# FFN work per iteration derived from TensorE's attention steps, in a top-k attention kernel with a SwiGLU block behind it

## The chip, the cores and the metric

The kernel runs on one core of a Trainium2 chip. Times are device microseconds of one execution. Before the change the median of three runs is 1890.77 us (1890.12 to 1893.95). The profile is of one execution of 1892.5 us.

## The reference

Eight batches with eight heads each attend over 576 positions of 64 numbers. Of each row of scores only the 32 largest count. The result, laid out as 4608 tokens of 512 numbers, goes through a gated FFN.

```python
def _attn_ref(q, k, v):                      # q, k, v: (8, 8, 576, 64)
    scores = scale * np.matmul(q, k.transpose(0, 1, 3, 2))
    kth = np.partition(scores, -top_k, axis=-1)[..., -top_k:-top_k + 1]
    mask = scores >= kth                     # top_k = 32
    scores = np.where(mask, scores, -1000000000.0)
    scores = scores - np.max(scores, axis=-1, keepdims=True)
    attn = np.exp(scores)
    attn = attn / (np.sum(attn, axis=-1, keepdims=True) + 1e-09)
    return np.matmul(attn, v).astype(np.float32)

def _moe_ref(x, w_gate, w_val, w_out):       # x: (4608, 512), d_ff 1536
    g = x @ w_gate
    silu = g * (1.0 / (1.0 + np.exp(-g)))
    val = x @ w_val
    return (silu * val @ w_out).astype(np.float32)
```

## The kernel before

The program is one long sequence. It is cut into 160 units: batch, query tile, pair of heads. Tiles 0 to 3 hold 128 queries, and such a unit has two rows of scores per partition, one for each head. Tile 4 (`qt == J`) holds the last 64 queries; the two heads share the partitions, and there is one row.

```python
units = [(b, qt, hp) for b in range(B) for qt in range(J + 1) for hp in range(NHP)]   # J = 4, NHP = 4

def n_heads(qt):
    return 1 if qt == J else 2
```

The main loop is a software pipeline over the units. In iteration n VectorE selects the 32 largest of unit n, while TensorE transposes the weights of unit n - 3 (`turn`), multiplies those of unit n - 4 with v (`values`), and makes the scores of unit n + 1 (`scores`). Before a new batch it also transposes keys and queries (`fetch`, for unit n + 2 with `qt == 0`). All engines take their instructions in the order in which the loop writes them down.

```python
TURN, VALUES = 3, 4
for n in range(NU + VALUES):                 # NU = 160
    nh = n_heads(units[n][1]) if n < NU else 1
    ...
    if n >= NU - NHP:
        credit[0] = 8.0
    else:
        credit[0] = min(credit[0] + (4.45 if nh == 2 else 2.25), 8.0)
    flush(on_act)
    if 0 <= n - 1 < NU:
        penalize(n - 1)                      # GpSimd
    flush(on_pool)
    if 0 <= n - TURN < NU:
        run(turn(n - TURN))                  # TensorE transposes, ScalarE copies
    if n >= VALUES:
        finish_unit(n - VALUES)              # TensorE: weights times v
    next(nxt, None)                          # TensorE: scores of n + 1
    if 0 <= n - 1 < NU:
        weigh(n - 1)                         # ScalarE: exp
    run(nxt)                                 # ScalarE: copies of the scores
    dve(2, beside=False)                     # VectorE: steps of select(n)
    ...
    pieces(2)
    ...
    dve(1)
    dve(1)
    next(norm, None)                         # VectorE: 1 / sum of unit n - 2
    run(norm)                                # ScalarE: weights of unit n - 2, scaled
    next(ahead, None)                        # TensorE: keys and queries of a new batch
    pieces(1)
    next(ahead, None)
    dve(1)
    pieces(1)
    dve(2)
    run(topk)
    pieces(6)
while piece():
    pass
```

Beside attention, TensorE works through the FFN in pieces. A piece of the gate or value product is four matmuls and costs 1 credit; a piece of the output product, which is done in seven quarter products, is three matmuls and costs 0.75. A block of 256 tokens has 24 pieces of the first kind and 14 of the second (block 0: 12 pieces of the plain output product, at 1 each). A block can begin only when all its tokens have their attention. Where no block is ready, `piece()` returns 0 and the credit is kept, up to 8.

```python
def pieces(n):
    for _ in range(n):
        if credit[0] >= 1:
            credit[0] -= piece()

def piece():
    ...
    while True:
        if not current:
            if not todo or done.get(todo[0], 0) < NHP * BLK:   # BLK = 256
                return 0
            ...
            current.append(feed(todo.pop(0)))
        cost = next(current[0], 0)
        ...
        return cost
```

The instructions that the profile names by line: 297 and 283 are the matmuls of scores of a full and a half unit, 302 and 288 the ScalarE copies of these scores out of PSUM; 318 is VectorE's maximum of eight, the first of which in a unit reads the scores (`m<-sc`), and 322 its replacement of what was found; 340 is GpSimd's adding of the penalty; 349 exp and 364 the scaling of the weights, both on ScalarE; 376 the transposes of weights; 396 and 405 weights times v; 459 the gate and value products; 545 the quarter products of the output.

Of the kernel before, what the change touches and what calls it, by code (L numbers as in the profile page):

```python
# [27 lines left out]
def kernel(  # L28
# [40 lines left out]
    J = S // P  # L69
# [64 lines left out]
    def weights():  # L134
# [11 lines left out]
        for n in range(len(pieces) + lags[0]):  # L146
            for lag in lags:
                if 0 <= n - lag < len(pieces):
                    next(pieces[n - lag], None)
            ready[0] = max(n - lags[0] + 1, 0)  # L150
            yield
# [38 lines left out]
    def rounding(n):  # L190
        for _ in range(n):
            next(weight, None)
# [9 lines left out]
    def load(i):  # L202
        b, hp = pairs[i]
        h = slice(2 * hp, 2 * hp + 2)
        kq = ld.tile([P, 2, J, 2, D], FP32, tag="kq", name="kq_in")
        kq_last = ld.tile([P, 2, D], FP32, tag="kql", name="kq_last")
        for n, src in ((0, k), (1, q)):
            queue = nc.scalar if n == 1 and i == 0 else nc.sync
            for hh in range(2):
                queue.dma_start(  # L210
                    kq[:, n, :, hh, :],
                    src[b, 2 * hp + hh, 0:JP].rearrange("(p j) d -> p j d", j=J),
                )
            queue.dma_start(
                kq_last[n * R : (n + 1) * R], src[b, h, JP:S].rearrange("h p d -> p h d")
            )
        raw[i] = (kq, kq_last)
# [42 lines left out]
    units = [(b, qt, hp) for b in range(B) for qt in range(J + 1) for hp in range(NHP)]  # L260
    state = {}

    def n_heads(qt):

        return 1 if qt == J else 2

    def scores(n):
        b, qt, hp = units[n]
        slab = preps[b * NHP + hp]
        sc = work.tile([P, 2 * S], FP32, tag="sc", name="sc", bufs=2)  # L270
        halves = [slice(0, D), slice(D, P)]
        half = S // 2

        def bank():
            return ps_t.tile([P, 512], FP32, tag="t", name="s")


        if qt == J:
            banks = [bank() for _ in range(2)]
            for i, ps in enumerate(banks):  # L280
                for d in halves:
                    k0 = R + i * half
                    nc.tensor.matmul(  # L283
                        ps[d, 0:half], slab[d, S + R : S + 2 * R], slab[d, k0 : k0 + half]
                    )
            yield
            for i, ps in enumerate(banks):
                nc.scalar.copy(sc[:, i * half : (i + 1) * half], ps[:, 0:half])  # L288
        else:
            q0 = S + 2 * R + qt * P  # L290
            banks = []
            for i in range(2):
                for hh, d in enumerate(halves):
                    ps = bank()
                    banks.append((i + 2 * hh, ps))
                    k0 = (1 - hh) * R + i * half
                    nc.tensor.matmul(  # L297
                        ps[:, 0:half], slab[d, q0 : q0 + P], slab[d, k0 : k0 + half]
                    )
            yield  # L300
            for i, ps in banks:
                nc.scalar.copy(sc[:, i * half : (i + 1) * half], ps[:, 0:half])  # L302
        state[n] = dict(sc=sc)

    def select(n):

        nh = n_heads(units[n][1])
        sc = state[n]["sc"]
        m = small.tile([P, 2, TOP_K], FP32, tag="m", name="m", bufs=2)
        heads = [slice(t * S, (t + 1) * S) for t in range(nh)]  # L310
        rest = work.tile([P, 2 * S], FP32, tag="rest", name="rest", bufs=1)
        e = work.tile([P, 2 * S], FP32, tag="e", name="e", bufs=4)
        state[n] |= dict(m=m, e=e, heads=heads)
        cur = sc
        rounds = TOP_K // 8
        for r in range(rounds):
            for t, hs in enumerate(heads):
                nc.vector.max(m[:, t, 8 * r : 8 * r + 8], cur[:, hs])  # L318
                yield
            if r < rounds - 1:  # L320
                for t, hs in enumerate(heads):
                    nc.vector.match_replace(  # L322
                        rest[:, hs], m[:, t, 8 * r : 8 * r + 8], cur[:, hs], LOWEST
                    )
                    yield
                cur = rest
        for t, hs in enumerate(heads):
            nc.vector.tensor_scalar(  # L328
                e[:, hs], sc[:, hs], m[:, t, TOP_K - 1 : TOP_K], FAR, ALU.is_lt, ALU.mult
            )  # L330

    def penalize(n):

        st = state[n]
        sc, m, e, heads = st.pop("sc"), st.pop("m"), st["e"], st["heads"]
        nh = len(heads)
        bias = small.tile([P, 2], FP32, tag="bias", name="bias")
        nc.gpsimd.tensor_scalar_mul(bias[:, 0:nh], m[:, 0:nh, 0], -scale)
        every = slice(0, nh * S)
        nc.gpsimd.tensor_tensor(e[:, every], e[:, every], sc[:, every], ALU.add)  # L340
        st["bias"] = bias
# [15 lines left out]
    def normalize(n):  # L357
        st = state[n]
        tot, e, heads = st.pop("tot"), st["e"], st.pop("heads")
        nh = len(heads)  # L360
        nc.vector.reciprocal(tot[:, 0:nh], tot[:, 0:nh])  # L361
        yield
        for t, hs in enumerate(heads):
            nc.scalar.mul(e[:, hs], e[:, hs], tot[:, t : t + 1])  # L364
# [76 lines left out]
    def flush(queue):  # L441
        while queue:
            queue.pop(0)()
# [182 lines left out]
    NU = len(units)  # L626
# [3 lines left out]
    def piece():  # L630

        if len(on_act) > 1:
            flush(on_act)
        if len(on_pool) > 1:
# [3 lines that stand above are left out]
                if not todo or done.get(todo[0], 0) < NHP * BLK:  # L638
# [5 lines that stand above are left out]
            if cost == 0:  # L644
                current.pop()
                continue
            return cost

    def fetch(n):

        b, qt, hp = units[n]
        i = b * NHP + hp
        if qt == 0:
            yield from prep(i)
        if qt == J and i + NHP < len(pairs):
            load(i + NHP)

    def pieces(n):
        for _ in range(n):
            if credit[0] >= 1:  # L660
                credit[0] -= piece()

    def run(steps):
        for _ in steps:
            pass

    def finish_unit(n):
        values(n)
        b, qt, hp = units[n]
        if qt == J and b + 1 < B:  # L670
            load_v((b + 1) * NHP + hp)
# [7 lines left out]
    credit = [0.0]  # L679
    no = iter(())  # L680
    over = {}
    TURN, VALUES = 3, 4
    due = [0.0]
    for n in range(NU + VALUES):
        nh = n_heads(units[n][1]) if n < NU else 1
        topk = select(n) if n < NU else no
        over[n - 1] = normalize(n - 1) if 0 <= n - 1 < NU else no
        nxt = scores(n + 1) if n + 1 < NU else no
        ahead = fetch(n + 2) if n + 2 < NU else no
        norm = over.pop(n - 2, no)  # L690

        def dve(k, beside=True):

            for _ in range(k * nh):
                next(topk, None)
                due[0] += 5 / 11 if beside else 0
                if due[0] >= 1:
                    due[0] -= 1
                    rounding(1)

        if n >= NU - NHP:
            credit[0] = 8.0
        else:
            credit[0] = min(credit[0] + (4.45 if nh == 2 else 2.25), 8.0)
        flush(on_act)
        if 0 <= n - 1 < NU:
            penalize(n - 1)
        flush(on_pool)
        if 0 <= n - TURN < NU:
            run(turn(n - TURN))  # L710
        if n >= VALUES:
            finish_unit(n - VALUES)
        next(nxt, None)
        if 0 <= n - 1 < NU:
            weigh(n - 1)
        run(nxt)

        dve(2, beside=False)
        if 2 <= n + 2 < NHP:
            load(n + 2)  # L720
        if n < NHP:
            load_v(n)
# [5 lines that stand above are left out]
        next(norm, None)  # L728
        run(norm)
# [8 lines that stand above are left out]
# [50 lines left out]
```

## Time and profile before

| | before |
|---|---|
| median of 3 runs | 1890.77 us |
| span of the profiled execution | 1892.5 us |
| granted TensorE clock, mean | 0.955 |
| MAX8 over scores or rest (line 318) | 1152 instructions, 615.2 + 205.4 us |
| gate and value matmuls (line 459) | 3456 records, 404.8 + 397.9 us |
| output product's quarters (line 545) | 1428 records |

In the page's first part each engine has its busy time, its share of the span and its count of instructions: PE is TensorE's matmuls, PEld its weight loads, DVE VectorE, ACT ScalarE, POOL GpSimd. In the second part each digit is the busy share of one fortieth of the span in tenths, and PEclk is the clock that TensorE was granted. A line of the list of waits reads: the engine and line that waited, the engine and line that ended the wait, microseconds in all, how often, the longest. A line of the timeline gives the start and length of a run of like instructions, and in brackets the idle time before it and what ended it.

### The profile page before, as it was taken

How to read it: one execution, taken by the hardware profiler on the slowest of the kernel's cores; microseconds unless marked ns; L12 is line 12 of the kernel's file. 1: busy time of each engine (PE TensorE's matmuls, PEld its weight loads, DVE VectorE, ACT ScalarE, POOL GpSimd, SP SyncE). 2: the span in 40 equal slices, each digit the busy share in tenths (PEclk: the TensorE clock that was granted, in tenths of full speed). 3: DMA queues.
4: the chain of work that ended last, by engine and by line, in shares of the span. 5: the costliest groups of instructions: out<-in, count | busy, mean ns of one | idle time of the engine just before them, and what ended most of it. 6: DMA issues, size and time to landing. Idle time of an engine off the chain costs nothing.

```text
span 1892.5 us, 30875 instructions
## 1 busy us (share of the span) xinstructions
PE 1723.2 (91%) x10756; PEld 1419.1 (75%) x10756; DVE 1632.0 (86%) x3477; ACT 1212.3 (64%) x3015; POOL 1023.2 (54%) x1007
## 2 busy tenths in 40 slices
PE   3446789989999999899899999999999999899998
PEld 2335658868888878787788888878888878787877
DVE  7998789999999989997899989999899989999300
ACT  5656666667666666675667666766676767666531
POOL 4555656636455546555364655554646554546534
PEclk7668899989999999899999999999999999999989
DMA  7222212000300012000210003000210001000000
GB/s 186 84 84 78 67 27 69 1 12 2 78 12 12 1 28 64 12 1 13 52 38 1 12 3 82 7 12 1 53 38 12 1 14 46 18 1 12 1 12 12
DMA packets 111260, 59.67 MB, mean 32 GB/s; under 512 B 89088, under 2 KB 97280, under 8 KB 111104
## 3 DMA queue, kind: packets, MB, share of 16 engines
q1 hardware_dynamic: 109904, 57.41, 11.6%
q8 instruction: 85, 1.39, 0.3%
q14 instruction: 71, 0.58, 0.1%
q10 hardware_dynamic: 1200, 0.30, 0.1%
HBM read 48.23 MB, written 9.44 MB: 30 GB/s over the span
## 4 chain that ended last, share of the span: by engine, by line
PE 79%; ACT 7%; POOL 7%; DVE 4%; issue 2%; DMA 0%; SPq 0%; POOLq 0%; ACTq 0%
PE f L459 38%; PE av L405 8%; PE x_ps L545 8%; PE etps L376 8%; PE s L297 6%; PE y_ps L545 5%; POOL e L340 3%; ACT e L349 2%; PE s L283 2%; ACT sc L302 2%; PE av L396 1%; DVE m L318 1%; DVE rest L322 1%; PE kqps L252 1%; PE o_ps L505 1%
## 5 line engine op out<-in xcount | busy, mean ns | idle before, releaser
L318 DVE MAX8 m<-rest 128x8 f32<-128x576 f32 x864 | 615.2, 747 | 2.2
L322 DVE MATCH_REPLACE8 rest<-m,rest 128x576 f32<-128x576 f32 x576 | 423.9, 742 | 0.0
L340 POOL TENSOR_TENSOR e<-e,sc 128x1152 f32<-128x1152 f32 (+1 forms) x160 | 382.7, 2392 | 59.4 <-DVE e L328 59.0
L459 PE MATMUL f<-xT,wg 128*128 128x256 f32 x1728 | 404.8, 385 | 0.0
L459 PE MATMUL f<-xT,wv 128*128 128x256 f32 x1728 | 397.9, 381 | 0.0
L459 PEld LDWEIGHTS f<-xT,wg 128*128 128x128 f32 x1728 | 324.4, 191 | 66.7 <-issue 23.7
L459 PEld LDWEIGHTS f<-xT,wv 128*128 128x128 f32 x1728 | 324.3, 190 | 55.6 <-issue 13.5
L487 POOL TENSOR_TENSOR h<-h,half_g 128x512 f32<-128x512 f32 x108 | 138.0, 1278 | 385.9 <-ACT h L486 377.4
L318 DVE MAX8 m<-sc 128x8 f32<-128x576 f32 x288 | 205.4, 749 | 127.1 <-ACT sc L288 70.9
L376 PE MATMUL etps<-ident,e 128*128 128x128 f32 (+1 forms) x1312 | 191.0, 291 | 132.2 <-POOL size L116 48.1
L349 ACT ACTIVATE e<-e,bias 128x576 f32<-128x576 f32 x288 | 222.0, 776 | 114.6 <-POOL e L340 114.6
L376 PEld LDWEIGHTS etps<-ident,e 128*128 128x128 f32 (+1 forms) x1312 | 161.9, 150 | 163.9 <-POOL size L116 51.3
L377 ACT COPY et<-etps 128x512 f32<-128x512 f32 (+1 forms) x448 | 185.0, 483 | 126.5 <-PE etps L376 124.9
L492 POOL TENSOR_TENSOR h<-h,val 128x512 f32<-128x512 f32 x108 | 140.0, 1296 | 160.8 <-ACT val L491 160.8
L364 ACT ACTIVATE e<-e,tot 128x576 f32<-128x576 f32 x288 | 211.5, 787 | 5.3 <-DVE tot L361 5.1
L322 DVE MATCH_REPLACE8 rest<-m,sc 128x576 f32<-128x576 f32 x288 | 211.8, 741 | 0.0
L297 PE MATMUL s<-kqT 64*128 64x288 f32 x1024 | 175.5, 451 | 9.1 <-ACT kqT L257 5.8
L328 DVE TENSOR_SCALAR e<-sc,m 128x576 f32<-128x576 f32 x288 | 173.4, 639 | 3.4
L405 PE MATMUL av<-et,v 128*64 128x128 f32 (+1 forms) x2560 | 176.3, 284 | 0.0
L302 ACT COPY sc<-s 128x288 f32<-128x288 f32 x512 | 163.9, 402 | 3.3 <-PE s L297 3.3
L484 ACT ACTIVATE h<-f 128x512 f32<-128x512 f32 x108 | 65.2, 603 | 149.8 <-PE f L459 149.8
L405 PEld LDWEIGHTS av<-et,v 128*64 128x64 f32 x2560 | 139.2, 147 | 23.4 <-issue 7.9
(71 smaller groups left out, 2042.6 us busy)
## 6 DMA issues: line engine op xcount, KB each, us to landing
kq_in<-in_k_dram SPq DMA_DIRECT2D x64, 128.0 KB, 2.8
v<-in_v_dram SPq DMA_DIRECT2D x32, 256.0 KB, 3.0
kq_in<-in_q_dram SPq DMA_DIRECT2D x62, 128.0 KB, 2.9
w<-in_moe_w_gate_dram SPq DMA_DIRECT2D x24, 256.0 KB, 2.7
w<-in_moe_w_val_dram SPq DMA_DIRECT2D x24, 256.0 KB, 2.7
w<-in_moe_w_out_dram SPq DMA_DIRECT2D x24, 256.0 KB, 2.6
out_dram<-o SPq DMA_DIRECT2D x40, 128.0 KB, 2.4
out_dram<-o SPq DMA_DIRECT2D x16, 256.0 KB, 2.4
```

Of the source, the lines that this page charges most:

```text
L297: nc.tensor.matmul(ps[:, 0:half], slab[d, q0 : q0 + P], slab[d, k0 : k0 + half])
L302: nc.scalar.copy(sc[:, i * half : (i + 1) * half], ps[:, 0:half])
L318: nc.vector.max(m[:, t, 8 * r : 8 * r + 8], cur[:, hs])
L322: nc.vector.match_replace(rest[:, hs], m[:, t, 8 * r : 8 * r + 8], cur[:, hs], LOWEST)
L340: nc.gpsimd.tensor_tensor(e[:, every], e[:, every], sc[:, every], ALU.add)
L349: nc.scalar.activation(e[:, hs], e[:, hs], AF.Exp, bias=bias[:, t : t + 1], scale=scale, accum_out=tot[:, t : t + 1],)
L364: nc.scalar.mul(e[:, hs], e[:, hs], tot[:, t : t + 1])
L376: nc.tensor.transpose(ps[0:kl, c * P : (c + 1) * P], e[:, k0 : k0 + kl], ident[:])
L377: nc.scalar.copy(et[0:kl, c0 : c0 + cn, :], ps[0:kl, 0 : cn * P].rearrange("p (c j) -> p c j", c=cn),)
L405: nc.tensor.matmul(av[hh * R : (hh + 1) * R, 0:ql], v_last[:, hh, :] if c == J else vt[:, hh, c, :], moving, start=last and c == 0, stop=c ...
L459: nc.tensor.matmul(ps[:, i, :], w[:, kc, m * P : (m + 1) * P], x[:, kc, :], start=(kc == 0), stop=(kc == KC - 1),)
L545: nc.tensor.matmul(ps, lhsT, T[i][m], start=m == 0, stop=m == MQ - 1)
```

## The change

The credit that an iteration receives was a constant: 4.45 with two rows of scores, 2.25 with one. Now it is worked out: 6.5 for the time of the unit's selection on VectorE (half of it with one row), less the cost of the attention steps that TensorE has in this iteration: 0.7 for the scores of the next unit, 0.6 for the transposes, 0.7 for the values (each halved where that unit has one row), and 0.6 where keys and queries of a new batch are transposed. So an iteration whose own unit is short, but whose TensorE steps belong to full units, gets fewer pieces. The last four units and the cap of 8 are as before.

```diff
+    def share(n):
+
+
+        others = 0.0
+        for m, cost in ((n + 1, 0.7), (n - TURN, 0.6), (n - VALUES, 0.7)):
+            if 0 <= m < NU:
+                others += cost * (0.5 if units[m][1] == J else 1)
+        if units[n + 2][1] == 0:
+            others += 0.6
+        return 6.5 * n_heads(units[n][1]) / 2 - others
+
     def pieces(n):
         for _ in range(n):
             if credit[0] >= 1:
@@ -701,7 +712,7 @@
         if n >= NU - NHP:
             credit[0] = 8.0
         else:
-            credit[0] = min(credit[0] + (4.45 if nh == 2 else 2.25), 8.0)
+            credit[0] = min(credit[0] + share(n), 8.0)
         flush(on_act)
         if 0 <= n - 1 < NU:
             penalize(n - 1)
```

## The prediction, made before the changed kernel was run

> Units are numbered in the order in which the program takes them: unit 20b + 4t + h is batch b, query tile t (0 to 4), head pair h. Tile 4 is the one of the last 64 queries, so units 16 to 19 of each batch hold one row of scores per partition where the others hold two. I call these four half units and the other sixteen full ones. An iteration is one turn of the main loop, iteration n the one in which VectorE selects for unit n. A credit is the kernel's own unit of FFN work: a piece of gate or value product is 1, a piece of the output product 0.75.
>
> **What bounds the kernel now.** I read the page's busy shares and slices first, then the waits of VectorE, then the windows of stretches whose ends are starts of units (the start of a unit's first maximum over the scores), then TensorE's timeline where it stood still.
>
> ```profile
> PE 1723.2 (91%) x10756; PEld 1419.1 (75%) x10756; DVE 1632.0 (86%) x3477; ACT 1212.3 (64%) x3015; POOL 1023.2 (54%) x1007
> ...
> PE   3446789989999999899899999999999999899998
> DVE  7998789999999989997899989999899989999300
> ...
> PEclk7668899989999999899999999999999999999989
> ...
> DVE m L318 <- ACT sc L288: 70.9, 24, 11.0
> DVE m L318 <- ACT sc L302: 55.4, 41, 4.2
> ```
>
> TensorE and VectorE are both nearly full from the eighth slice on. VectorE's waits are 126 us in all, and more than half of them (70.9 us in 24 waits) are in front of half units: line 288 is the copy of a half unit's scores. That is the loss the change aims at. But those scores come late because TensorE is at its FFN pieces, so the question is how much TensorE itself stands still. The windows (columns: stretch, its length, busy time of PE, PEld, DVE, ACT, POOL, then granted clock) answer that:
>
> ```profile
> 759.40:771.70 12.30, 11.24 (x71) 9.16 (x69) 10.76 (x25) 6.50 (x18) 10.71 (x12) 1.00 0.00 1
> 771.70:782.20 10.50, 6.59 (x42) 5.46 (x43) 10.50 (x23) 8.07 (x21) 2.65 (x3) 0.72 0.14 52
> ...
> 457.10:491.70 34.60, 34.60 (x239) 28.40 (x238) 27.07 (x49) 23.31 (x61) 24.08 (x29) 1.00 0.10 22
> ...
> 884.50:926.90 42.40, 37.23 (x246) 29.66 (x245) 26.16 (x50) 27.03 (x65) 16.32 (x15) 1.00 0.08 18
> 402.00:782.20 380.20, 372.97 (x2410) 310.55 (x2407) 355.01 (x741) 258.00 (x642) 208.66 (x192) 0.99 0.11 26
> ...
> 873.90:1265.50 391.60, 377.75 (x2433) 312.72 (x2435) 352.72 (x741) 261.76 (x647) 209.53 (x194) 0.99 0.11 27
> 1265.50:1646.20 380.70, 373.46 (x2422) 311.01 (x2424) 355.34 (x741) 259.06 (x645) 208.65 (x192) 0.99 0.09 23
> ```
>
> The first two are units 65 and 66, the next two are four half units each (36 to 39 and 76 to 79), the last three the stretches of units 31 to 66, 75 to 110 and 111 to 146. In the long stretches TensorE is busy 98, 96 and 98%. In the half units 36 to 39 it is busy throughout while VectorE has 27.07 us of work in 34.60. So the binding engine is TensorE, and VectorE's waits are the shadow of its queue. Where TensorE does stand still is units 65 and 66:
>
> ```profile
> 767.78 2.86 PE L545 MATMUL x_ps<-wo,h 128*128 128x256 f32 x12
> 772.60 2.00 PE L376 MATMUL etps<-ident,e 128*128 128x128 f32 x9 [1.96 <-ACT e L364]
> 774.39 0.63 PE L396 MATMUL av<-et,vlast 128*128 128x128 f32 x2
> 774.95 1.76 PE L405 MATMUL av<-et,v 128*64 128x128 f32 x16
> 776.64 1.24 PE L297 MATMUL s<-kqT 64*128 64x288 f32 x8
> 780.89 2.15 PE L376 MATMUL etps<-ident,e 128*128 128x128 f32 x9 [3.01 <-issue]
> ```
>
> There is no FFN matmul between 770.6 and 787: the block of 256 tokens is finished and the next one's tokens are not. TensorE waits 1.96 and 3.01 us for weights of attention, and what it does then is at a lower clock (the nine transposes take 2.0 us, and 0.98 us elsewhere). By the trace the same happens at units 109/110 (1.96 and 2.10 us) and 145/146 (1.97 and 3.01 us).
>
> **What the Trainium skill says.** "TensorE: Matmul & The Clock Gate", Part 1, says that the clock gate drops to half rate after an idle window of about 3.4 us and needs a busy one to come back. The trace agrees: the granted clock is 0.72 in the stretch of unit 66, and around units 65, 109 and 145 it is at one half for 10.2, 6.8 and 3.4 us. "Perfetto Trace Analysis", Identifying the Most-Contended Engine, warns that matmul occupancy is a poor measure and weight-load occupancy a better one for TensorE; here weight loads are at 82% of the long stretches (310.55 of 380.20), so I don't take "98% busy" as peak and check it by counting below. The same page, Optimization Strategy, advises interleaving regimes with different bounds; that is what the credits do.
>
> **The change part by part.** No operation is added or removed. VectorE's instructions keep their order entirely; on TensorE FFN pieces move between iterations, and the copies and products that follow a piece on ScalarE and GpSimd move with it.
>
> Sizes, from the chain of waits: 64 records of gate and value matmuls take 14.01 us, so a credit (8 records) is 1.75 us; 24 records of the output product take 5.18 us, so 0.75 credit is 1.30 us, the same rate. Full unit: transposes 0.98, values 0.22 + 1.02 = 1.24, scores about 1.2: 3.4 us. Half unit: 0.55, 0.90 and 1.12. Preparing keys and queries: nine transposes, 0.98. VectorE without waits takes 10.56 us for a full unit and 6.06 for a half one (their starts in the trace, where it doesn't wait).
>
> Before, a half iteration does the attention of two full units and one half one (0.98 + 1.24 + 1.12 = 3.3 us), 2.25 credits (3.9 us) and in two of four a preparation: 7.3, 7.3, 8.3 and about 8.0 us, 31 us against VectorE's 24.2. After, the formula gives 1.6, 1.6, 1.0 and 0.95 credits: 3.85 fewer, 6.7 us, so 24 us against 24.2. The three later full iterations get 4.55, 4.55, 5.15 and the next 4.85 instead of 4.45, the rest 4.5. A full iteration is then 3.4 + 4.5 x 1.75 = 11.3 us against 10.56, so TensorE is still the fuller one there: the work taken out of half units lands where there is no room for it. Over a batch 78.6 credits are granted where 80.2 were, and 77.6 are needed (2.25 blocks of 24 + 14 x 0.75 = 34.5).
>
> Walking the credit rule by hand through units 55 to 67:
>
> unit 55 56 57 58 59 60 61 62 63 64 65 66 67
> before 4.25 2 3 2 2 4 5 4 4.5 4.5 1.5 0 8
> after 4.75 2 1 1 1 5 4 5 4.75 4.5 4.5 0.75 8
>
> By the end of unit 66 both have done 208.5 credits: the block's end is fixed by its tokens. So nothing is gained by doing less in the half units as such; what changes is that TensorE runs dry in one iteration and not two. The pair 65/66 gets 5.25 credits instead of 1.5, 6.6 us more work in the place of the stall. The same holds at 109/110 and 145/146. At 28 to 30 it is 2.25, 0, 0 instead of 0.75, 0, 0; at 74 and 154 (0 instead of 0.75) nothing is won. From unit 155 on both are alike, the tail with its last block included.
>
> Upper limit: a stretch like 31 to 66 holds 138 credits (241.5 us), 28 full and 8 half units of attention (95 + 21) and 8 preparations (8): 366 us. The three stretches take 380.2, 391.6 and 380.7, so TensorE loses 14, 26 and 15 us in them, and no more than that is to be had. Of it the dry pairs account for 14.0 us idle (the six waits above) and about half of 20.5 us at half clock, 24 us in all, three times 8. With 6.6 us more work in each I expect about 5 of each 8 back: the last dry unit still has only 0.75 credits, 4.7 us of work in 10.56, but TensorE comes to it with a queue that VectorE had been waiting for. That is -15 us. The other idle time, in half units 57/58, 77 to 79, 98 and 137/138 (10 us in all), is TensorE waiting for weights of attention, and fewer pieces there may lengthen it as well as shorten it: 0, give or take 5. Units 20 to 30 are bound by VectorE (116 us of work in 120): at most 1 us. Sum: 1890.8 - 15 = 1876 us.
>
> **The rivals.** First: VectorE is the bound, and its 70.9 us of waits before half units disappear, some 50 net of what turns up elsewhere: 1840 us. For it speaks the wait list; against it TensorE's 98%. Second: pure shifting. The waits before half units move in front of full units (line 302), the dry units stay as costly because the fixed block ends force a burst of 8 credits right after, and the time stays at 1888 to 1892. For it speaks that the totals at units 66, 110 and 146 are equal. Third: the half iterations become too light for what TensorE waits for there. Its transposes need the weights of the unit three back, which need VectorE, GpSimd and ScalarE in turn; with one piece between attention steps each such wait is bare. With 2 to 3 us more in each of seven groups: 1895 to 1905. Against it: TensorE comes into a half unit with the 4.5 to 4.85 credits of the full one before it still ahead.
>
> **Range and chances.** The dry pairs can give from 6 to 24 us, and the half units -5 to +5, perhaps more: 1862 to 1888, with 1876 the middle. Faster by over 2% needs less than 1853, a saving of 38 us out of the 55 that TensorE loses in the three stretches, while half of that loss isn't touched: 0.06. Slower by over 2% would need the third rival several times over: 0.01.
>
> **What would show it.** If the reading is right: TensorE's busy time stays within 15 us of 1723; the waits of line 318 for line 288 fall from 70.9 to 35 to 50, those for line 302 rise from 55; the idle times at units 65, 109 and 145 are gone and half clock is seen in one short piece or none; the three stretches last about 375, 386 and 375 us; the last 157 us from unit 155 on are unchanged. The sum is wrong if the waits before half units fall and the time with them by far more than TensorE's idle time does (first rival), or if new waits of transposes for line 364 appear in half units (third).

## The result, and the profile after

The changed kernel takes 1898.42 us (median of 6 runs, 1897.68 to 1900.76), the kernel before 1891.2 us in the same series. The ratio is 1.0038, with a 95% interval from 1.0025 to 1.0051: it is slower by about 7 us. The prediction had 1876, and 1888 as the upper end.

The first view is the page of the changed kernel and its list of waits, as they were shown of before:

```profile
PE 1720.2 (91%) x10756; PEld 1414.8 (75%) x10756; DVE 1629.8 (86%) x3477; ACT 1212.8 (64%) x3015; POOL 1022.2 (54%) x1007
...
PE   3437789979999999999999999999999999999998
...
DVE  7998788999999989999899989999999989989300
...
PEclk7667889999999999999999999999999999999999
...
DVE m L318 <- ACT sc L302: 69.4, 55, 5.5
...
DVE m L318 <- ACT sc L288: 55.7, 20, 11.0
```

The work is what it was (TensorE 1720.2 us against 1723.2). VectorE's waits in front of half units fell from 70.9 to 55.7 us, and those in front of full units rose from 55.4 to 69.4: the sum is 125.1 us, and was 126.3. So the change did what it was meant to do to half units, and something else took it back.

Next are windows of the changed kernel. Their ends are again starts of units: 20 to 30, 36 to 39, 66, 76 to 79, then the three long stretches of units 31 to 66, 75 to 110 and 111 to 146:

```profile
281.40:411.00 129.60, 115.03 (x729) 91.30 (x729) 119.35 (x253) 81.83 (x207) 71.46 (x64) 0.97 0.12 31
466.30:496.50 30.20, 30.20 (x220) 24.50 (x219) 25.75 (x50) 22.68 (x61) 17.16 (x20) 1.00 0.11 24
...
777.10:788.40 11.30, 10.77 (x69) 8.74 (x67) 10.61 (x23) 6.70 (x19) 8.23 (x9) 1.00 0.00 0
892.20:927.80 35.60, 34.08 (x231) 26.88 (x230) 24.23 (x50) 25.73 (x62) 15.59 (x16) 1.00 0.09 20
411.00:788.40 377.40, 370.44 (x2401) 307.23 (x2397) 351.92 (x741) 255.89 (x638) 206.33 (x190) 1.00 0.10 25
881.70:1263.30 381.60, 374.42 (x2420) 309.99 (x2420) 352.04 (x741) 259.03 (x641) 207.58 (x192) 1.00 0.11 26
1263.30:1643.30 380.00, 371.63 (x2420) 308.48 (x2420) 354.03 (x741) 259.24 (x645) 208.00 (x192) 1.00 0.09 23
```

and one of the kernel before, its units 20 to 30:

```profile
282.40:402.00 119.60, 112.27 (x719) 90.96 (x719) 117.77 (x253) 82.28 (x207) 69.27 (x64) 0.95 0.13 34
```

The three long stretches are shorter than before, by 2.8, 10.0 and 0.7 us. The half units take 30.2 instead of 34.6 us (36 to 39) and 35.6 instead of 42.4 (76 to 79). Unit 66 is no longer cold: its granted clock is 1.00, and was 0.72. But units 20 to 30 take 129.6 us instead of 119.6. There VectorE has the same work (119 and 118 us), and the 10 us are nearly all waiting.

Of these 10 us, 6.3 come up in units 22 and 23, which take 13.3 and 16.1 us and took 12.5 and 10.6, and 3.7 in units 25 to 28. Where the first part comes from is seen on GpSimd in unit 23. First the changed kernel's GpSimd timeline, with the idle time before an instruction in brackets:

```profile
317.58 1.27 POOL L487 TENSOR_TENSOR h<-h,half_g 128x512 f32<-128x512 f32 x1 [3.31 <-ACT h L486]
318.82 1.30 POOL L171 TENSOR_TENSOR t<-wo 128x512 f32<-128x512 f32 x1
320.20 1.42 POOL L177 TENSOR_TENSOR t<-wo,t 128x256 f32<-128x256 f32 x2
321.58 1.27 POOL L167 TENSOR_TENSOR wo<-wo 128x512 f32<-128x512 f32 x1
322.93 1.30 POOL L171 TENSOR_TENSOR t<-wo 128x512 f32<-128x512 f32 x1
324.30 1.44 POOL L177 TENSOR_TENSOR t<-wo,t 128x256 f32<-128x256 f32 x2
325.69 0.43 POOL L338 TENSOR_SCALAR bias<-m 128x2 f32<-128x2 f32 x1
326.09 2.87 POOL L340 TENSOR_TENSOR e<-e,sc 128x1152 f32<-128x1152 f32 x1
```

and what follows from it on TensorE and VectorE, in their timelines:

```profile
331.94 0.76 DVE L318 MAX8 m<-sc 128x8 f32<-128x576 f32 x1 [5.46 <-ACT sc L302]
...
334.40 1.95 PE L376 MATMUL etps<-ident,e 128*128 128x128 f32 x9 [3.87 <-issue]
```

Then the same unit on GpSimd in the kernel before:

```profile
316.92 1.28 POOL L492 TENSOR_TENSOR h<-h,val 128x512 f32<-128x512 f32 x1 [2.57 <-ACT val L491]
318.17 0.20 POOL L338 TENSOR_SCALAR bias<-m 128x2 f32<-128x2 f32 x1
318.34 2.64 POOL L340 TENSOR_TENSOR e<-e,sc 128x1152 f32<-128x1152 f32 x1
```

Lines 167, 171 and 177 are sums over the output weights, twelve instructions that the kernel does once, for the quarter products. They may begin only when block 0 has used the plain weights. With the change the half units 16 to 19 of batch 0 get 5 credits and not 9, and 3 of block 0's and block 1's credits slip behind unit 20. So the sums start later: five of them lie in unit 22 and seven in unit 23, these behind a product (line 487) that itself waits for FFN results, and in front of line 340, the softmax step of unit 22. That step starts 11.5 us after VectorE has finished unit 22 (at 314.6). Exp waits for it, ScalarE's copies of the next scores are behind exp, and VectorE and TensorE wait in turn, 5.46 and 3.87 us. In the kernel before six of the sums lie in unit 20 and six in unit 22, none in 23, and line 340 starts 3.2 us after VectorE was done with unit 22 (315.1). The second part of the 10 us has another source, which is shown with kernel 1 below.

### The profile page after: what moved, and what is told of

It reads as the page before. It is cut to its first block, busy times and chain, and to the rows that moved or that the text cites. A ratio compares the mean times of both kernels' runs of the same rounds, so it can differ in the third digit from the quotient of the medians.

```text
span 1895.5 us, 30885 instructions
## 1 busy us (share of the span) xinstructions
PE 1720.2 (91%) x10756; PEld 1414.8 (75%) x10756; DVE 1629.8 (86%) x3477; ACT 1212.8 (64%) x3015; POOL 1022.2 (54%) x1007
## 3 DMA queue, kind: packets, MB, share of 16 engines
q1 hardware_dynamic: 109904, 57.41, 11.6%
## 4 chain that ended last, share of the span: by engine, by line
PE 78%; ACT 7%; POOL 7%; DVE 5%; issue 2%; DMA 0%; POOLq 0%; SPq 0%; ACTq 0%; DVEq 0%
PE f L459 38%; PE x_ps L545 8%; PE av L405 8%; PE etps L376 7%; PE s L297 6%; PE y_ps L545 6%; POOL e L340 3%; ACT e L349 2%; DVE m L318 2%; PE s L283 2%; DVE rest L322 2%; ACT sc L302 2%; PE av L396 1%; POOL size L126 1%; PE kqps L252 1%
## 5 line engine op out<-in xcount | busy, mean ns | idle before, releaser
L459 PEld LDWEIGHTS f<-xT,wv 128*128 128x128 f32 x1728 | 325.7, 190 | 54.4 <-issue 11.4
L318 DVE MAX8 m<-sc 128x8 f32<-128x576 f32 x288 | 205.6, 751 | 134.4 <-ACT sc L302 69.4
```

The lines of the kernel that those rows point to most:

```text
L459: nc.tensor.matmul(ps[:, i, :], w[:, kc, m * P : (m + 1) * P], x[:, kc, :], start=(kc == 0), stop=(kc == KC - 1),)
```

## The experiments

To compare kernels I measure on TensorE: from the start of the score matmuls of one unit to those of another, the idle time between matmuls in that stretch, and the time in which the granted clock was one half. Between the scores of 32 and of 156 every kernel does nearly the same work, 483 credits and the same attention. Times are medians. The ratio is to the kernel before as run beside each, whose median was 1890.7 to 1893.1 us, and has its 95% interval; kernels of different series are compared by it. The other columns are from the profiled execution of each. How far the stretch from 20 to 32 can be trusted is seen where two kernels are the same up to unit 31: before, 5 and 9 show 122.9, 122.8 and 122.9 us, the change and 4 show 132.7 and 132.6.

| kernel | us | ratio | 20 to 32 | 32 to 156 | idle in it | half clock in it | rest |
|---|---|---|---|---|---|---|---|
| before | 1891.2 | 1 | 122.9 | 1336.5 | 32.8 | 25.3 | 1291.0 |
| the change | 1898.4 | 1.0038 (1.0025 to 1.0051) | 132.7 | 1331.5 | 32.8 | 10.5 | 1293.5 |
| 1 from batch 1 | 1897.7 | 1.0038 (1.0023 to 1.0053) | 129.5 | 1332.6 | 33.1 | 11.8 | 1293.6 |
| 2 only batch 0 | 1897.2 | 1.0029 (1.0018 to 1.0041) | 130.5 | 1331.9 | 32.8 | 13.9 | 1292.1 |
| 3 no sums | 1894.7 | 1.0008 (0.9995 to 1.0021) | 126.1 | 1333.4 | 32.7 | 15.9 | 1292.7 |
| 4 next unit | 1923.3 | 1.0170 (1.0150 to 1.0191) | 132.6 | 1355.0 | 44.2 | 37.5 | 1292.1 |
| 5 units 75 to 111 | 1887.6 | 0.9977 (0.9966 to 0.9988) | 122.8 | 1330.1 | 27.6 | 22.2 | 1291.4 |
| 6 even 20 to 30 | 1885.2 | 0.9972 (0.9959 to 0.9984) | 122.6 | 1327.5 | 28.4 | 9.9 | 1294.1 |
| 7 before, no sums | 1890.9 | 1.0003 (0.9991 to 1.0014) | 122.6 | 1331.7 | 32.9 | 13.7 | 1292.0 |
| 8 paced | 1869.2 | 0.9882 (0.9866 to 0.9898) | 125.4 | 1309.4 | 17.3 | 7.4 | 1288.4 |
| 9 paced from 31 | 1862.8 | 0.9835 (0.9818 to 0.9852) | 122.9 | 1306.4 | 16.1 | 5.1 | 1287.8 |
| 10 change, cap | 1872.4 | 0.9886 (0.9873 to 0.9900) | 120.6 | 1322.3 | 23.4 | 10.2 | 1293.8 |
| 11 constants, cap | 1894.3 | 1.0012 (1.0003 to 1.0021) | 123.8 | 1332.6 | 27.6 | 13.7 | 1298.2 |
| 12 more in half | 1865.6 | 0.9843 (0.9827 to 0.9860) | 125.2 | 1305.1 | 11.6 | 10.2 | 1288.4 |
| 13 before, copies first | 1903.2 | 1.0065 (1.0052 to 1.0078) | 126.4 | 1339.9 | 37.8 | 18.8 | 1292.6 |
| 14 change, copies first | 1907.6 | 1.0090 (1.0075 to 1.0106) | 134.6 | 1340.3 | 38.0 | 15.3 | 1294.7 |
| 15 paced, copies first | 1876.7 | 0.9926 (0.9914 to 0.9939) | 126.3 | 1315.4 | 20.0 | 11.5 | 1289.6 |

"Rest" is the length less the idle time and less half of the half-clock time (half, as nine transposes took 2.00 us at half clock in unit 66 and take 0.98 elsewhere). It is the reading that the table is for: from 1287.8 to 1294.7 in all kernels but one. In this part of the program TensorE's work is fixed, and a kernel's time is that work plus what TensorE stands still or runs slow. The half-clock time is not a property of a program alone: kernels 2 and 7 have the TensorE order of the kernel before in this stretch, and show 13.9 and 13.7 us where its own profile has 25.3.

**1 and 2: which batch.** Theory A: the loss is made in batch 0. Theory B: the half units of all batches are too light.

```diff
-            credit[0] = min(credit[0] + share(n), 8.0)
+            credit[0] = min(credit[0] + (share(n) if n >= 20 else (4.45 if nh == 2 else 2.25)), 8.0)
```

> The derived credits from unit 20 on, the constants in batch 0. Theory A (the change loses its time in the first batch only: with fewer credits in units 16 to 19 the first FFN block ends later, and GpSimd's sums over the output weights, which wait for it, land in front of the softmax work of units 22 and 23): stretch from the scores of unit 20 to those of 32 as before, 123 us instead of 132.7, and the later stretches keep what the profile of the change shows (-5 to -8 us), so 1882 to 1887 us. Theory B (the half units of all batches are too light for TensorE): 1895 to 1899 us.

```diff
+            credit[0] = min(credit[0] + (share(n) if n < 20 else (4.45 if nh == 2 else 2.25)), 8.0)
```

> The mirror: derived credits in units 0 to 19 alone, the constants from unit 20 on. Theory A: 8 to 11 us slower than before, 1899 to 1902 us, all of it between the scores of units 20 and 32. Theory B: within 2 us of before, 1889 to 1893 us.

Each half of the change costs as much as the whole, about 6 us. That fits neither theory. The traces agree with A on the place: 1 loses 6.6 us between 20 and 32, 2 loses 7.6 there, and from 32 on neither differs from the change (1332.6, 1331.9, 1331.5). But A had the reason too narrow. Kernel 1 gives block 0 its old credits, and its sums lie where they lay before (the first at 282.4 us, the last at 309.5), and still it loses. The formula hands the first units of batch 1 more: 6 credits in unit 22 and 4.25 in 25 instead of 5 and 3.75, and then 0 in 28. Of the 6.6 us, 5.6 come up in units 26 and 27, which take 13.4 and 13.8 us and took 11.0 and 10.6. GpSimd's timeline shows what stands there in front of the softmax step of unit 25:

```profile
352.31 1.28 POOL L492 TENSOR_TENSOR h<-h,val 128x512 f32<-128x512 f32 x1 [5.00 <-ACT val L491]
353.54 2.11 POOL L552 TENSOR_TENSOR xT<-h 128x256 f32<-128x256 f32 x3
355.60 2.12 POOL L560 TENSOR_TENSOR h<-h 128x256 f32<-128x256 f32 x3
357.67 0.23 POOL L338 TENSOR_SCALAR bias<-m 128x2 f32<-128x2 f32 x1
357.84 2.65 POOL L340 TENSOR_TENSOR e<-e,sc 128x1152 f32<-128x1152 f32 x1
```

VectorE was done with unit 25 at 349.3 us, so line 340 starts 8.5 us after it; in the kernel before it is 5.4. Lines 552 and 560 are sums for block 1's own output product, in front of its first and its third piece. In kernel 1 iteration 25 has 2 credits of gate and value product and then 2.25 of output product, so both sums come in front of line 340; before it had 3 and 0.75, and only line 552 did. Kernel 2 has the pattern of 2 and 2.25 in iteration 26 and takes 13.4 and 13.8 us in units 27 and 28; its other loss is in unit 23, which has seven of the sums in it and takes 14.9 us.

**3 and 7: the sums.** The sums of lines 167, 171 and 177 are left out, in the change and in the kernel before; the output product then uses the plain weights, and only the time is of use.

```diff
-            nc.gpsimd.tensor_tensor(t1, t1, wo[:, mm, lo], sub)
...
-            nc.gpsimd.tensor_tensor(t2[:], wo[:, nn, hi], t1, sub)
-            T[6] += [t2[:, i, :] for i in range(2)]
+            T[6] += [wo[:, MQ + m + i, lo] for i in range(2)]
...
-                nc.gpsimd.tensor_tensor(t4[:], wo[:, MQ + m + i, lo], t2[:, i, :], sub)
-                T[4].append(t4[:])
+            T[4] += [wo[:, MQ + m + i, lo] for i in range(2)]
```

> The change as it is, but GpSimd's sums over the output weights after block 0 are left out (nine instructions of line 167 to 177 or fifteen with the double ones; the output product uses the plain weights in their place). Theory A: the stretch from unit 20 to 32 shrinks from 132.7 to 120 to 125 us, total 1887 to 1892 us. If the stretch stays at 130 or more, the sums are not the cause and the pieces themselves are.

> The kernel before with GpSimd's sums left out as in the run on the change without them, where the stretch from unit 20 to 32 shrank by 6.6 us to 126.1. Theory D: before loses nothing to the sums, the stretch stays at 121 to 123 us. Theory C: it shrinks too, by 2 to 5 us, and stays some 6 to 8 us below the change without sums.

In the change the stretch falls from 132.7 to 126.1 us, in the kernel before from 122.9 to 122.6: the sums cost nothing where they lay, and 6.6 us where the change put them. GpSimd's timeline in unit 23 of kernel 3 (its lines are numbered 9 lower) shows the softmax step directly behind the product that waits:

```profile
313.28 1.28 POOL L478 TENSOR_TENSOR h<-h,half_g 128x512 f32<-128x512 f32 x1 [5.37 <-ACT h L477]
314.53 0.21 POOL L329 TENSOR_SCALAR bias<-m 128x2 f32<-128x2 f32 x1
314.71 2.63 POOL L331 TENSOR_TENSOR e<-e,sc 128x1152 f32<-128x1152 f32 x1
```

What is left, 126.1 against 122.6, has the 3 credits (5.2 us of TensorE's time) in it that moved behind unit 20, and with them block 1's output product, which begins in iteration 26 with 3.75 credits behind 1 (before in 25 with 0.75 behind 3). Line 340 of units 26 and 27 starts 6.1 and 8.7 us after VectorE; before it was 2.8 and 5.5.

**4: the next unit's time.** A form of theory B: the pieces of iteration n lie beside the selection of n + 1.

```diff
+        beside = n + 1 if n >= 20 else n
-        return 6.5 * n_heads(units[n][1]) / 2 - others
+        return 6.5 * n_heads(units[beside][1]) / 2 - others
```

> The change, but from unit 20 on the selection time in the formula is that of unit n + 1 and not n (the pieces of iteration n are queued behind the scores of n + 1, so they lie beside the selection of n + 1). The sum of credits is the same. Theory B (TensorE stands still in the second to fourth half unit and in the first full one behind them, 1.4 to 4.7 us per batch in the profile of the change, because light iterations meet a long selection): these idle times fall to under 1 us per batch, 1886 to 1892 us. Theory A alone: 1896 to 1900 us, as the change.

It is 25 us slower than the change, so this other alignment is no remedy; whether the formula's own is at fault stays open. Idle time grew to 44.2 us: at most places the unit before the half ones now gets 2 credits or less, and TensorE stands still 2.2 us at units 36 and 116 and 4.4 us at 55 and 135, most of it in front of transposes.

**5 and 6: where it gains, and the repair of units 20 to 30.** Theory C: from 32 on the change is a wash but for the half units behind a burst of 8 credits (76 to 80); in units 20 to 30 VectorE is the bound, and each of its waits is lost. Theory D: the sums alone.

```diff
+            credit[0] = min(credit[0] + (share(n) if 75 <= n < 112 else (4.45 if nh == 2 else 2.25)), 8.0)
```

> The derived credits only in units 75 to 111, the constants everywhere else. Theory C (from unit 32 on the change is a wash: TensorE's idle time moves from the dry pairs into light half units and the full unit behind them; it gains only where half units follow a burst of 8 credits, units 76 to 80, and it loses in units 20 to 31): the stretch between the scores of 76 and 112 takes 380 to 381 us instead of 387.9, all others as before, so 6 to 8 us faster than before, about 1884 to 1886. If the gain in that stretch is given back behind unit 112: as before, 1890 to 1892.

```diff
+            credit[0] = min(credit[0] + (min(share(n), 3.6) if 20 <= n < 31 else share(n)), 8.0)
```

> The change, but with at most 3.6 credits in units 20 to 30: the same 39.5 credits are spread over all eleven units there, GpSimd's sums stay. Theory C (this stretch is bound by VectorE, 116 us of selection, and it runs dry at units 28 to 30 anyway, so every wait that early heavy iterations cause VectorE is lost): 118 to 122 us between the scores of 20 and 32 instead of 132.7, total 1884 to 1889. Theory D (GpSimd's sums alone delay the softmax there, whatever the credits): 127 to 132 us, total 1893 to 1898.

Both came out as C has it (76 to 112 takes 381.5 us in 5), though 5 gained 4 us and not 6 to 8. Kernel 6 has all of the change, the sums and the 3 late credits, and only spreads the pieces:

```profile
280.80:399.00 118.20, 112.01 (x711) 88.82 (x709) 118.20 (x253) 80.26 (x203) 70.74 (x63) 0.99 0.12 30
```

That is the window of its units 20 to 30: 118.20 us long with VectorE busy for 118.20. It never waits, against 129.60 with 119.35 in the change. So neither the sums nor the credits cost anything there as such. With the pieces the sums moved as well, to 294 to 318 us; but in kernel 10 below they lie as in the change (from 303.8 and from 319.5 us on, and there from 304.6 and 318.8), line 340 of units 21 to 28 starts at most 1.4 us after VectorE, and the stretch takes 120.6 us. So D falls: what costs is heavy iterations with the sums, or with the start of block 1's output product, on top of them. The whole is 13 us faster than the change.

**8 and 9: constants that use up the stretch.** The fixed credit is set so that the pieces of a stretch last until its end.

```diff
+            credit[0] = min(credit[0] + (3.6 if 20 <= n < 31 else 4.31 if nh == 2 else 2.25), 8.0)
```

> The kernel before with other constants and no formula: 3.6 credits in units 20 to 30, else 4.31 in full units instead of 4.45, 2.25 in half ones. The blocks' pieces then spread to the end of each stretch and TensorE runs dry in one unit instead of two, and after bursts of 7 and not 8. Theory C: 118 to 120 us for units 20 to 32 (before 122.9); dry idle at 65/66, 109/110 and 145/146 falls from 14 us to about 6 while the half units keep their 2.25 credits and so no new idle time: 1875 to 1882. If idle time only moves here too: 1886 to 1890.

```diff
+            full = 4.45 if n < 31 else 4.31
+            credit[0] = min(credit[0] + (full if nh == 2 else 2.25), 8.0)
```

> The constants of before up to unit 30, from 31 on 4.31 in full units and 2.25 in half ones. It parts the 22 us of the paced kernel. Theory C (dry units and the bursts of 8 behind them cost TensorE its time in the stretches from 32 on): units 20 to 32 as before, 123 us, all later stretches as in the paced kernel: 1867 to 1872 us. If half of the gain came from units 20 to 30: 1878 to 1884.

Number 9 is the fastest of all, 1862.76 us, with number 12 within the noise of it. It takes only the second part of 8, as 3.6 credits in units 20 to 30 cost 2.5 us more than they brought. The windows of its three long stretches:

```profile
402.90:774.10 371.20, 368.89 (x2403) 307.29 (x2399) 350.14 (x742) 256.27 (x638) 206.22 (x190) 1.00 0.10 25
864.80:1240.70 375.90, 370.56 (x2420) 308.29 (x2420) 353.07 (x741) 259.03 (x641) 207.94 (x191) 1.00 0.11 26
1240.70:1614.30 373.60, 369.92 (x2420) 308.40 (x2420) 352.24 (x741) 259.47 (x645) 207.92 (x192) 1.00 0.09 23
```

TensorE is busy 98.6 to 99.4% of each. They are 9.0, 15.7 and 7.1 us shorter than in the kernel before. In the table the idle time falls by 16.7 us, and the half-clock time by 20.2 (by 8.8 against kernel 2), of which half counts.

**10, 11 and 12: share against constants, without bursts.** A lower cap on saved credit keeps a dry unit from being followed by a burst.

```text
10: share(n), at most 3.6 in units 20 to 30, cap 5.2
11: 4.35 full (3.6 in units 20 to 30), 2.25 half, cap 5.0
12: 4.15 full (3.6 in units 20 to 30), 3.1 half, cap 5.0
```

> The change, with at most 3.6 credits in units 20 to 30 and a cap of 5.2 on saved credit instead of 8, so that no unit is dry and no burst over 5 follows. What is left is the derived share against constants, to be compared with the next run (constants, same cap). Theory B' (light half units leave TensorE idle, in them and in the full unit behind): idle time of 1.5 to 5 us per batch there, and 4 to 10 us slower than the constants with the cap, 1868 to 1874. If the share is right once bursts are gone: no idle there, and 3 to 8 us faster than the constants, 1857 to 1863.

> Constants with a cap of 5 on saved credit: 3.6 in units 20 to 30, else 4.35 in full units, 2.25 in half ones. No unit is dry, no burst. Theory C: dry idle time gone, units 76 to 80 take 44 us instead of 54; 1860 to 1867 us. If bursts don't matter: 1868 to 1870 as the paced kernel with the cap of 8.

> The opposite of the change: 3.1 credits in half units and 4.15 in full ones (3.6 in units 20 to 30), cap 5. If the share of half units is of little weight while TensorE is the bound: within 4 us of the constants with the cap. If VectorE's waits in half units are the loss, as the change supposes: 6 to 12 us slower than those.

Here C failed for number 11: no unit is dry, no burst follows, and it takes 1894.33 us, 30 more than expected. Its idle time is 27.6 us, spread over places such as 3.3 us at units 56 and 136 and 1.1 us each at 49, 67, 111 and 147, in front of transposes that wait for line 364; its rest is 1298.2, the only one that stands out, and from the scores of 156 to the end it takes 156.1 us where most take 152 to 153. Number 12, the opposite of the change, is one of the best. So dry units are a loss, but taking them away isn't enough. What marks out number 11 is the passage seen in kernel 1: in 12 of its 14 blocks from unit 31 on, the output product begins behind 1 or 2 credits of gate and value product, with 2.25 or more of its own in the same iteration. Before it is 5 of 14, in the change 4, in number 12 3, in 8 and 9 none.

**13, 14 and 15: ScalarE's order.** In the traces most of the time that VectorE waits in front of full units lies behind the moment when the scores are ready in PSUM: some 47 of 52 us before, 61 of 65 with the change, 27 of 37 in kernel 9 (units 20 to 155). ScalarE is at exp, or waits to begin it until GpSimd is through with line 340. Theory E: this order is the cause. Theory F: TensorE is the bound, and such waits are its shadow.

```diff
-        if 0 <= n - 1 < NU:
-            weigh(n - 1)
         run(nxt)
+        if 0 <= n - 1 < NU:
+            weigh(n - 1)
```

> The kernel before, but ScalarE copies the scores of unit n + 1 ahead of the exp of unit n - 1. Theory E (VectorE's waits in front of full units come from ScalarE's order: the copies stand behind an exp that waits for GpSimd): the waits of line 318 for line 302 fall from 55 to under 20 us, and the time by 25 to 45 us, 1846 to 1866. Theory F (TensorE is the bound, the waits are its shadow and only change their name): within 8 us of before, 1883 to 1899.

> The change with the same turn. Theory E: it gains more than before does, as it has 61 us of such waits and not 47, and no longer stands behind it: 1840 to 1862, at or below the other run. Theory F: 1890 to 1900. If the half units are too light in themselves, it stays 5 us or more above the kernel before with the turn.

> The paced kernel (4.31 from unit 31 on) with the same turn. Theory E: it has only 27 us of such waits, so it gains less, 10 to 20 us: 1843 to 1853, and the three come close to one another. Theory F: 1858 to 1866.

All three became slower, by 12, 10 and 17 us by the ratios, so E falls. The waits in the list of kernel 13:

```profile
DVE m L318 <- ACT sc L288: 78.7, 23, 10.9
DVE m L318 <- ACT sc L302: 42.9, 24, 4.2
```

In front of full units they fell from 55.4 to 42.9, and in front of half ones they rose from 70.9 to 78.7. Between units 20 and 155 the part with the scores ready fell from 71 to 27 us, and the part in which VectorE waits for TensorE itself rose from 23 to 61. Now it is exp that comes late, TensorE's transposes wait for it, and its idle time rose from 32.8 to 37.8 us. F holds in sense, though its upper figures were 4, 8 and 11 us too low: the turn is not neutral, it takes TensorE's inputs away.

## Why the prediction was wrong

The step that failed is the one on units 20 to 30, put as "bound by VectorE (116 us of work in 120): at most 1 us". I took a stretch with little to gain for one with little to lose. On TensorE's measure it lost 9.8 us: 6.6 from the sums, which the prediction never looked at, and the rest with the 3 credits that left the half units of batch 0 and moved block 1's output product. In both, GpSimd comes late with the softmax step (11.5 and 8.7 us behind VectorE in units 22 and 27), and the scores that VectorE needs are copied only after it. None of the rivals had it either. Kernel 6 shows that the loss lies in how the pieces fall there: with them spread, the change is 0.9972 of before, faster by a little.

The dry pairs came out as to mechanism and too small as to size. The idle time at 65/66, 109/110 and 145/146 fell from 14.0 to 5.9 us. In the profiles the half-clock time from 32 to 156 fell from 25.3 to 10.5, but kernel 2, with the order of the kernel before there, shows 13.9, so only 3.4 us of it can be put down to the change, and half of that counts. So the term of 15 us is about 10.

The half units, put at 0 give or take 5, took back 5.9 us of that, in the places that the third rival names. Idle time in half units and in the full unit behind them (and in 101 before) went from 11.4 to 17.3 us: in the change TensorE stands still at 57/58, 97/98 and 137/138 and again at 40, 60, 100, 120 and 140, where the iteration before has given it 0.75 or 1 credit. Two more places that I counted as neutral, 74 and 154 with 0 credits instead of 0.75, went from 5.9 to 8.7. That light iterations are the reason is not shown: at 77 to 79 they came with less idle time (1.5 us after 5.2), and kernel 11, with 2.25 credits in each half unit, has 18.3 us in these places. The sum from 32 to 156 is 32.8 us before and after, which is the second rival, a pure shift. In length, too, nothing was gained there: 1331.5 us, against 1331.9 in kernel 2, which has TensorE's order of before there. Of the 13.5 us by which the three long stretches are shorter, units 67 to 74 and 147 to 154 gave back 7.4 (93.3 and 94.9 us for 91.7 and 89.1), and much of the rest is the half clock of that one profile.

Right was, from unit 32 on, that TensorE is the bound and VectorE's waits its shadow (table; kernel 13), with the listed marks: busy time within 15 us of 1723 (1720.2), line 288 down, though to 55.7 and not to 50, line 302 up, half clock gone from units 65 and 109, and the end from unit 155 on unchanged (157.1 and 157.4 us). Of the stretches 375, 386 and 375 us were expected; 377.4, 381.6 and 380.0 were measured. Two slips of the working change nothing: a half unit without waits takes 6.25 us from start to start in the trace, not 6.06, and iteration 15 gets 4.85 credits too, which its sum of 78.6 has and its list has not.

Not settled is what in kernel 11 leaves TensorE idle for 27.6 us without a dry unit, why an even 3.6 in units 20 to 30 helps the change and not the paced constants, and how much of the gain of 8 and 9 comes from the pace. Where the blocks' output products begin goes with the first and the last, but kernel 4 has only 4 of the 14 such passages and is the slowest, and no run here varied that alone.

## What to carry to other kernels

Where a scheduler shares out filler work, count what it leaves of the bound engine's idle time over the whole stretch between two points that it can't move. If the filler's supply is fixed, less of it in one place is more in another, and only idle time that ends is gained. Here a constant 3% lower, with which the supply lasts longer, brought 1.65%, but it also moved the starts of the output products, and no run parts the two; a formula that balanced each iteration brought a loss. And look at the one-time work that hangs on the filler's progress: on an engine that takes its instructions in order, twelve small sums cost nothing in one place and 6.6 us in another, 15 to 31 us later.

## What the runs showed of the hardware that was not expected

The clock fell to one half behind short gaps. In the kernel before the gap at unit 65 is 1.96 us (770.6 to 772.6), and the granted clock is at one half from 772.9 on for 3.4 us; around the next, of 3.01 us, it is so for 6.8 us. With the change there is a gap of 1.96 us at unit 66 too, and no half clock. The prediction took its trace to agree with an idle window of about 3.4 us; the gaps around units 65, 109 and 145, behind which the clock fell, are 1.96 to 3.01 us long. The same order of TensorE's instructions gave 25.3 us of half clock in one kernel's profile and 13.9 in another's. So a few idle microseconds may cost two or three more, or nothing.
